# A two-level second product: long VectorE sums moved behind short ones, and the last results stored by quarters

## The chip, the cores and the metric

The kernel runs on one core of a Trainium2 chip. The core has five engines, each with its own queue of instructions: TensorE (PE; its weight loads are shown as PEld), VectorE (DVE), ScalarE (ACT), GpSimd (POOL) and SyncE (SP), which only issues transfers. The engines wait for each other through semaphores; an engine carries out its own queue strictly in order. The metric is the device time of one execution in microseconds; of several executions the median is taken.

## The reference

Attention with normalised queries and keys, followed by a feed-forward block with a squared ReLU, all in 32-bit floats:

```
q_n, k_n = rmsnorm(q, g_q), rmsnorm(k, g_k)          # 8 batches, 12 heads, 448 positions, 64 wide
attn = softmax(q_n @ k_n.T / sqrt(64))
x = (attn @ v) -> (3584, 768)                        # 8 * 448 rows, 12 * 64 columns
h = x @ w_in                                         # (3584, 2048)
out = (maximum(h, 0) ** 2) @ w_out                   # (3584, 768)
```

The last line is the second product. The change concerns its last part alone.

## The kernel before, in words

The eight batches are worked in four spans of two. In each span attention fills `xT`, the first product turns it into `gT` (sixteen chunks of 128 rows of the hidden layer, and 2 x 448 columns, one half for each batch), and the second product turns `gT` into output. Both products use a scheme with seven block products in place of eight: the matrices are cut into two by two blocks, and sums and differences of blocks are multiplied. The sums of weights are made once; the differences of activations for the second product are made by `combine` (L1021), four VectorE subtractions of 128x448 for each chunk, which fill `gC` and one half of `gT`. In the first three spans the second product runs beside the attention of the next span. For the last span there is no attention left, and `last_product` (L1144) does it. It is the function that changes.

`last_product` goes through the seven block products in the order A11, A12, S2, S1, S3, A22, S4 (L1148), here called block product 0 to 6, and each of them is done by the same scheme a second time, on blocks of half the size. Each has three row blocks of 128 output rows (m = 0, 1, 2). Row blocks 0 and 1 are done by the inner scheme; row block 2 ("third", L1228) is a plain product. For one block product TensorE runs, in this order, eight groups: `pa` (a11 b11), `ps` (row block 2, sixteen matmuls of 448 columns), `pb` (s2 t2), `pc` (s1 t1), `pd` (s3 t3), and then adds onto three of these: `pa` again (a12 b21), `pd` again (a22 t4), `pc` again (s4 b22). Each of the small groups has eight matmul records of 224 columns. An accumulator that is added onto has to be read in between, where its first content alone is needed:

- L1261: ScalarE copies the first `pa` to `p1i`;
- L1273 and L1277: VectorE makes `zi` from `p1i` and `pb`, and `yi` from `zi` and the first `pc`;
- L1283 to L1287: VectorE's `meet` (its work stands at L1244) takes the first `pd` into the second half of row block 1; only then may the second `pd` group start, since it adds onto the same bank;
- L1290 or L1292, L1294, L1300: the same for the second `pa`, `pd` and `pc`. These are 128x224 and short.

The long VectorE work is `add_g(o, n)` (L1185, its subtraction at L1191): for each block product o four differences t1 to t4 of 128x896, from the eight chunks of that block's activations. They alternate between two sets of places, so those of block product o + 1 may be made while o runs. The sums of weights s1 to s4 of the next block product are GpSimd's (`add_weights`, L1173, its work at L1179), and the weights themselves come by one transfer of 1.5 MB (`load_set`, L1168, issued by SP).

The order in the queues is the order of the program text: nothing reorders it. Ahead of `last_product`'s first group, in the last two steps of the last first_product, VectorE is given add_g(0, 0) to add_g(0, 3) and half of combine for the last chunk (L1387 to L1393). Then each block product o gives it, in this order: add_g(o + 1, 0) to (o + 1, 2) (L1262), the stores held over from the block product before, row block 2's sum (L1238), `zi`, `yi`, add_g(o + 1, 3) (L1278), and the `meet`s. The other half of that combine follows at the end of block product 0 (L1308).

Finished output leaves by `deliver` (L1137): VectorE transposes a 128x448 tile in squares of 32 into `osb` (L1139), and four transfers of 32 partitions each write it out (L1142). In block product 6 (`end`) the transfers alternate between the queues of SP and ScalarE, row block 1 is stored as a whole once both its halves are done, and row block 0 in two halves (L1296 to L1303).

Of the kernel before, what the change touches and what calls it, by code (L numbers as in the profile page):

```python
# [387 lines left out]
def attention_then_ffn_bounded(  # L388
# [37 lines left out]
    B, H, S, D = q.shape  # L426
# [9 lines left out]
    HF = NFC // 2  # L436
# [23 lines left out]
    def bank(name, n=None):  # L460

        turn[0] += n is None
        return ps_m.tile([P, S], F32, tag="mn"[turn[0] % 2 if n is None else n], name=name)
# [557 lines left out]
    def combine(f, parts=(0, 1)):  # L1021


        g11, g12 = gT[:, f, 0:S], gT[:, f, S:2 * S]
        g21, g22 = gT[:, HF + f, 0:S], gT[:, HF + f, S:2 * S]
        sub = nc.vector.tensor_tensor
        if 0 in parts:
            sub(gC[:, 0, f], g12, g11, ALU.subtract)
            sub(gC[:, 1, f], g22, gC[:, 0, f], ALU.subtract)
        if 1 in parts:  # L1030
            sub(gC[:, 2, f], g21, gC[:, 1, f], ALU.subtract)
            sub(g12, g22, g12, ALU.subtract)
# [111 lines left out]
    def last_product(pool):  # L1144
# [4 lines left out]
        HK, HS = HF // 2, S // 2  # L1149
# [7 lines left out]
        ts = [[t[:, n * NT2:(n + 1) * NT2].rearrange("p (c n) -> p c n", c=HK) for n in range(4)] for t in (cf, xf)]  # L1157
        dead = [gT[:, f, 0:S] for f in range(HF)] + [gC[:, 1, f] for f in range(HF)]
        late = []
        sub, add = ALU.subtract, ALU.add  # L1160

        def weights_of(o, m, k):
            return sets[o % 2].rearrange("p (k c n) -> p k c n", k=2, c=HK)[:, k, :, m * P:(m + 1) * P]

        def sums_of(o):
            return [t.rearrange("p (c n) -> p c n", c=HK) for t in left[o % 2]]
# [14 lines left out]
        def parts_of(o):  # L1181
            rhs = rhs_of[order[o]]
            return [[rhs[:, k * HK:(k + 1) * HK, t * HS:(t + 1) * HS] for t in range(2)] for k in range(2)]

        def add_g(o, n):  # L1185
            if o == len(order):
                return
            (b11, b12), (b21, b22) = parts_of(o)
            t1, t2, t3, t4 = ts[o % 2]
            dst, x, y = ((t1, b12, b11), (t2, b22, t1), (t3, b22, b12), (t4, b21, t2))[n]  # L1190
            nc.vector.tensor_tensor(dst, x, y, sub)  # L1191

        def small_of(name):
            return work.tile([P, HS], F32, tag=name, name=name, bufs=1)
# [8 lines left out]
        def run(ps, lhs, rhs, first=True):  # L1203
            for c in range(HK):
                nc.tensor.matmul(ps, lhs[:, c], rhs[:, c], start=first and c == 0, stop=c == HK - 1,  # L1205
                                 skip_group_check=not first)

        turn[0] += 1
        for o, i in enumerate(order):
            end = o + 1 == len(order)  # L1210
            (b11, b12), (b21, b22) = parts_of(o)
            (a11, a12), (a21, a22) = [[weights_of(o, m, k) for k in range(2)] for m in range(2)]
            s1, s2, s3, s4 = sums_of(o)
            t1, t2, t3, t4 = ts[o % 2]

            into = {A11: [(None, p1s)], A12: [(p1s, None)], S2: [(p1s, p1s)], S1: [(p1s, ys)],
                    S3: [(ys, None), (p1s, p1s)], A22: [(p1s, None)], S4: [(ys, None)]}[i]
            leaves = any(dst is None for _, dst in into)
            into = [(base, dst or homes[i]) for base, dst in into]
            at = ((HC if i in (S3, A22) else 0), 1 if i in (S3, S4) else 0)  # L1220

            def send(m, part=slice(0, S // 32)):
                deliver(work, NSPAN - 1, into[0][1][m], m + at[0], at[1],
                        (nc.sync, nc.scalar) if end else (nc.sync,), part, 5)

            both = len(into) > 1

            def third():  # L1228
                m = HC - 1
                ps = bank("ps")  # L1230
                for c in range(HF):
                    nc.tensor.matmul(ps, weights_of(o, m, c // HK)[:, c % HK], rhs_of[i][:, c],  # L1232
                                     start=c == 0, stop=c == HF - 1)
                for base, dst in into:
                    if base is None:
                        nc.scalar.copy(dst[m], ps)
                    else:
                        nc.vector.tensor_tensor(dst[m], base[m], ps, add)  # L1238

            def meet(m, t, left, ps):  # L1240

                part = slice(t * HS, (t + 1) * HS)
                dst = blocks[m] if both else into[0][1][m]
                nc.vector.tensor_tensor(dst[:, part], left, ps, add)  # L1244

            def based(m, t, x, name):
                base = into[0][0]
                if both or base is None:
                    return x
                y = small_of(name)  # L1250
                nc.gpsimd.tensor_tensor(y, x, base[m][:, t * HS:(t + 1) * HS], add)
                return y

            def settle(m):
                for base, dst in into if both else ():
                    nc.gpsimd.tensor_tensor(dst[m], base[m], blocks[m], add)

            pa = ps_s.tile([P, 2, 512], F32, tag="s", name="pa")[:, 0, 0:HS]
            run(pa, a11, b11)
            p1 = small_of("p1i")  # L1260
            nc.scalar.copy(p1, pa)  # L1261
            for n in range(3):  # L1262
                add_g(o + 1, n)
            for args in late:
                deliver(*args)
            late[:] = []
            third()
            if leaves:
                send(HC - 1)
            pb = ps_o.tile([P, S], F32, tag="o", name="pb")[:, 0:HS]  # L1270
            run(pb, s2, t2)
            z, y = small_of("zi"), small_of("yi")
            nc.vector.tensor_tensor(z, p1, pb, add)  # L1273
            z21, z12 = based(1, 0, z, "za"), based(0, 1, z, "zb")
            pc = bank("pc")[:, 0:HS]
            run(pc, s1, t1)
            nc.vector.tensor_tensor(y, z, pc, add)  # L1277
            add_g(o + 1, 3)  # L1278
            pd = ps_o.tile([P, S], F32, tag="t", name="pd")[:, 0:HS]
            run(pd, s3, t3)  # L1280
            add_weights(o + 1)
            if both or into[0][0] is None:
                meet(1, 1, y, pd)  # L1283
            else:
                meet(1, 1, into[0][0][1][:, HS:S], pd)
                x = into[0][1][1][:, HS:S]
                (nc.vector if end else nc.gpsimd).tensor_tensor(x, x, y, add)  # L1287
            run(pa, a12, b21, False)
            if both or into[0][0] is None:
                nc.scalar.copy((blocks if both else into[0][1])[0][:, 0:HS], pa)  # L1290
            else:
                meet(0, 0, into[0][0][0][:, 0:HS], pa)  # L1292
            run(pd, a22, t4, False)
            meet(1, 0, z21, pd)  # L1294
            settle(1)
            if end:  # L1296
                send(1)
                send(0, slice(0, HS // 32))
            run(pc, s4, b22, False)
            meet(0, 1, z12, pc)  # L1300
            settle(0)
            if end:
                send(0, slice(HS // 32, S // 32))  # L1303
            elif leaves:
                for m in (1, 0):
                    late.append((work, NSPAN - 1, into[0][1][m], m + at[0], at[1], (nc.sync,), slice(0, S // 32), 5))
            if o == 0:
                combine(HF - 1, (1,))  # L1308
            load_set(o + 2)
        yield  # L1310

# [66 lines left out]
    with tc.tile_pool(name="last_product", bufs=2, reuse_waits="tile") as last:  # L1378
        rest = last_product(last)
        load_set, add_weights, add_g = next(rest)  # L1380
        with tc.tile_pool(name="first_product", bufs=2, reuse_waits="tile") as work:
            for u, _ in enumerate(first_product(work, NSPAN - 1)):
                if u in (14, 21):
                    load_set(u // 7 - 2)
                if u == N1 // 2:
                    add_weights(0)
                if u == N1 - 2:  # L1387
                    add_g(0, 0)
                    add_g(0, 1)
                if u == N1 - 1:  # L1390
                    add_g(0, 2)
                    add_g(0, 3)
                    combine(HF - 1, (0,))  # L1393
        with tc.tile_pool(name="second_product", bufs=2, reuse_waits="tile") as work:
            rest.send(work)

# [2 lines left out]
def kernel(  # L1399
# [49 lines left out]
    with tc.If(bits <= limit) as small_scores:  # L1449
        with tc.manual_schedule():  # L1450
            attention_then_ffn_bounded(tc, *args, held)
# [32 lines left out]
```

## Time and profile before

| what | time |
|---|---|
| median of 7 runs | 1359.15 us (1357.55 to 1360.98) |
| profiled execution, its own time | 1363.34 us |
| its span, first to last instruction | 1361.0 us |
| granted TensorE clock, mean | 0.995 |
| TensorE busy / VectorE busy | 1333.8 us / 877.5 us |
| first matmul of last_product | 1230.23 us after the span's start |
| first matmul of block product 1 | 1251.47 us |
| first matmul of block product 6 | 1334.84 us |
| last VectorE instruction | 1352.14 to 1352.55 us |

All times inside the kernel are counted from the span's start, in one profiled execution. The page of the profile lists how long each engine was busy, then the chain of work that ended last, followed back from the last instruction: the share of an engine or line in it says how much of the time it decided. The timeline has a row for each instruction, or run of like ones, with the idle time before it and the instruction that ended that idle time in brackets. A table of stages gives the busy time of each engine in a stretch of time, and then PEclk, the share of full clock that TensorE was granted in it. For transfers, "to landing" is the time from issue to completion.

### The profile page before, as it was taken

The page shows a single profiled execution, that of the slowest core. Times are in us where ns is not written, and L with a number is a line of the kernel's source. Part 1 is how long each engine was busy: PE and PEld are TensorE (multiplying, and loading weights), DVE is VectorE, ACT ScalarE, POOL GpSimd, SP SyncE. Part 2 cuts the span into 40 slices and gives each one's busy share as a digit, 9 for nine tenths or more (in the row PEclk, how much of TensorE's full clock was granted, in tenths as well). Part 3 has the DMA queues.
Part 4 walks back from the last instruction along what each step waited for, and adds up shares of the span by engine and source line. Part 5 has one row for each costly group of instructions (what it writes and reads, how often), then busy time and mean ns, then how long its engine had stood idle before and what let it go on. Part 6 is the DMA issues. An engine that isn't in the chain of part 4 may idle for free.

```text
span 1361.0 us, 17239 instructions
## 1 busy us (share of the span) xinstructions
PE 1333.8 (98%) x5770; PEld 670.6 (49%) x5770; DVE 877.5 (64%) x1536; ACT 431.7 (32%) x681; POOL 620.2 (46%) x504
## 2 busy tenths in 40 slices
PE   7999999999999999999999999999999999999997
PEld 3333445444444455444444455444444445556886
DVE  5999788599987433568787623457788733336552
ACT  6877466533332012233332111223333211110000
POOL 5666533455664122646555222446556312323452
PEclk8999999999999999999999999999999999999999
DMA  9687899656676333355685432345665435321333
GB/s 237 186 255 198 287 367 328 191 123 116 131 155 127 101 88 88 100 119 105 145 152 119 114 94 87 98 106 124 135 126 117 107 97 167 100 81 47 113 103 54
DMA packets 413814, 190.15 MB, mean 140 GB/s; under 512 B 282388, under 2 KB 408724, under 8 KB 413716
## 3 DMA queue, kind: packets, MB, share of 16 engines
q1 hardware_dynamic: 406164, 180.21, 51.4%
q0 software_dynamic: 4736, 8.40, 2.4%
q8 instruction: 48, 0.79, 0.2%
q10 hardware_dynamic: 2816, 0.34, 0.2%
q14 instruction: 50, 0.41, 0.1%
HBM read 155.72 MB, written 33.16 MB: 139 GB/s over the span
## 4 chain that ended last, share of the span: by engine, by line
PE 88%; DVE 6%; ACT 2%; DMA 1%; issue 1%; POOL 0%; SPq 0%; DVEq 0%; POOLq 0%; ACTq 0%
PE ps L1106 28%; PE pd L1068 10%; PE pa L1068 10%; PE pc L1068 10%; PE sc L785 7%; PE pav L862 7%; PE pb L1068 5%; PE ps L1232 3%; PE pd L1205 2%; PE pc L1205 1%; PE pa L1205 1%; DVE gT L810 1%; ACT gT L797 1%; DMA gT<-in_moe_w_in_dram 1%; PE tot L876 1%
## 5 line engine op out<-in xcount | busy, mean ns | idle before, releaser
L1106 PE MATMUL ps<-gT,sw 128*128 128x448 f32 x576 | 225.8, 543 | 0.0
L1044 POOL TENSOR_TENSOR gT<-gT 128x448 f32<-128x448 f32 x96 | 94.1, 982 | 285.2 <-ACT gT L1040 285.2
L750 POOL TENSOR_TENSOR half<-half,mhalf 128x28 f32<-128x28 f32 x36 | 174.9, 4857 | 71.9 <-DVE half L749 68.6
L1106 PE MATMUL ps<-gC,sw 128*128 128x448 f32 x432 | 170.1, 543 | 0.0
L1106 PEld LDWEIGHTS ps<-gT,sw 128*128 128x128 f32 x576 | 107.5, 190 | 113.9 <-issue 110.3
L1068 PE MATMUL pa<-xT,sw 128*128 128x448 f32 x384 | 155.0, 540 | 0.6 <-ACT p L1072 0.6
L1040 ACT ACTIVATE gT<-gT 128x448 f32<-128x448 f32 x96 | 55.4, 577 | 313.5 <-DVE gT L1083 313.5
L1106 PEld LDWEIGHTS ps<-gC,sw 128*128 128x128 f32 x432 | 80.6, 190 | 86.3 <-issue 83.7
L787 ACT ACTIVATE pr<-sc 128x896 f32<-128x896 f32 x87 | 77.4, 915 | 124.0 <-PE sc L785 124.0
L785 PE MATMUL sc<-qkT 64*64 64x448 f32 (+1 forms) x1152 | 109.8, 496 | 0.0
L1068 PEld LDWEIGHTS pa<-xT,sw 128*128 128x128 f32 x384 | 72.8, 190 | 72.7 <-issue 70.6
L583 POOL TENSOR_TENSOR gC<-gC 128x384 f32<-128x384 f32 x64 | 76.2, 1208 | 62.2 <-DVE gC L579 60.4
L1083 DVE TENSOR_TENSOR gT<-z,pd 128x448 f32<-128x448 f32 x32 | 19.8, 620 | 97.8 <-PE pd L1068 97.6
L1068 PE MATMUL pd<-xT,sw 128*128 128x448 f32 x192 | 77.9, 542 | 1.3 <-DVE z L1075 1.3
L830 POOL DMA_DIRECT2D xT<-factors x72 | 38.0, 532 | 90.5 <-DMA factors<-square 54.4
L1068 PE MATMUL pd<-xC,sw 128*128 128x448 f32 x192 | 77.5, 540 | 1.3 <-DVE gT L1083 1.3
L1068 PE MATMUL pb<-xC,sw 128*128 128x448 f32 x192 | 77.5, 540 | 0.1
L1068 PE MATMUL pc<-xC,sw 128*128 128x448 f32 x192 | 77.4, 539 | 0.0
L1068 PE MATMUL pc<-xT,sw 128*128 128x448 f32 x192 | 77.4, 539 | 0.0
L752 POOL TENSOR_TENSOR qk<-qk,half 128x448 f32<-128x448 f32 x72 | 75.6, 1070 | 2.8
L862 PE MATMUL rest<-pr,vt 64*64 64x448 f32 x348 | 72.7, 537 | 0.0
L862 PE MATMUL pav<-pr,vt 64*64 64x448 f32 x348 | 72.7, 537 | 0.0
(233 smaller groups left out, 2167.5 us busy)
## 6 DMA issues: line engine op xcount, KB each, us to landing
sw<-w1s SPq DMA_DIRECT2D x224, 192.0 KB, 2.3
sw<-w2s SPq DMA_DIRECT2D x126, 256.0 KB, 3.3
w1s<-gC SPq DMA_DIRECT2D x8, 1344.0 KB, 7.2
w2s<-gC SPq DMA_DIRECT2D x8, 1344.0 KB, 6.3
out_dram<-osb SPq DMA_DIRECT2D x184, 56.0 KB, 1.8
qk<-in_q_dram SPq DMA_DIRECT2D x144, 56.0 KB, 3.7
qk<-in_k_dram SPq DMA_DIRECT2D x144, 56.0 KB, 3.0
xT<-factors POOLq DMA_DIRECT2D x72, 112.0 KB, 3.4
```

The lines of the kernel that those rows point to most:

```text
L583: nc.gpsimd.tensor_tensor(*[blocks_of(n)[:, place_of(n, i)] for i in (dst, x, y)], op)
L750: nc.gpsimd.tensor_tensor(half, half, mhalf, ALU.pow)
L752: nc.gpsimd.tensor_tensor(qkn[:, s], raw[:, s], half[:, s * NG:(s + 1) * NG].rearrange("p g -> p g ()").to_broadcast([P, NG, 32]), ALU.mult)
L785: nc.tensor.matmul(sc[part, h, 0:n], qkT[rows, 0, 1, keys], qkT[rows, 0, 0, of], start=True, stop=True)
L787: nc.scalar.activation(pr, sc[:, :, 0:n], AF.Exp)
L862: nc.tensor.matmul(into, vs[i][rows, h, c, :], probs[i, c][rows, h, :], start=(c == 0), stop=(c == NF), skip_group_check=True)
L1040: nc.scalar.activation(g, src, AF.Relu)
L1044: nc.gpsimd.tensor_tensor(g, g, g, ALU.mult)
L1068: nc.tensor.matmul(ps, stream[n + at][:, c], rhs[:, c], start=first and c == 0, stop=c == HC - 1, skip_group_check=not first)
L1106: nc.tensor.matmul(ps, stream[n][:, c % 4], rhs_of[i][:, c], start=c == 0, stop=c == HF - 1)
L1205: nc.tensor.matmul(ps, lhs[:, c], rhs[:, c], start=first and c == 0, stop=c == HK - 1, skip_group_check=not first)
L1232: nc.tensor.matmul(ps, weights_of(o, m, c // HK)[:, c % HK], rhs_of[i][:, c], start=c == 0, stop=c == HF - 1)
```

## The change

It has two parts. In block product 0 the long differences for block product 1 go behind the first `meet` that a TensorE group waits for, all four together, and the whole combine of the last chunk goes to the end of block product 0. In the later block products the order is as it was. In block product 6 row block 1 is delivered in two halves, too: its second half as soon as it is summed, its first half behind the second `pd`; the first half of row block 0 goes out behind the second `pa`. `former` and `latter` are the two halves of the 448 columns.

```
+        former, latter = slice(0, HS // 32), slice(HS // 32, S // 32)
...
             nc.scalar.copy(p1, pa)
-            for n in range(3):
+            for n in range(3 if o else 0):
                 add_g(o + 1, n)
...
             nc.vector.tensor_tensor(y, z, pc, add)
-            add_g(o + 1, 3)
+            if o:
+                add_g(o + 1, 3)
...
                 (nc.vector if end else nc.gpsimd).tensor_tensor(x, x, y, add)
+            if end:
+                send(1, latter)
+            if o == 0:
+                for n in range(4):
+                    add_g(1, n)
             run(pa, a12, b21, False)
             if both or into[0][0] is None:
                 nc.scalar.copy((blocks if both else into[0][1])[0][:, 0:HS], pa)
             else:
                 meet(0, 0, into[0][0][0][:, 0:HS], pa)
+            if end:
+                send(0, former)
             run(pd, a22, t4, False)
             meet(1, 0, z21, pd)
             settle(1)
             if end:
-                send(1)
-                send(0, slice(0, HS // 32))
+                send(1, former)
             run(pc, s4, b22, False)
             meet(0, 1, z12, pc)
             settle(0)
             if end:
-                send(0, slice(HS // 32, S // 32))
+                send(0, latter)
...
             if o == 0:
-                combine(HF - 1, (1,))
+                combine(HF - 1)
...
                 if u == N1 - 1:
                     add_g(0, 2)
                     add_g(0, 3)
-                    combine(HF - 1, (0,))
```

More of the change, by code (lines that the diff above doesn't have):

```diff
@@ L1159, in last_product @@
         late = []
+        former, latter = slice(0, HS // 32), slice(HS // 32, S // 32)
         sub, add = ALU.subtract, ALU.add
@@ L1261, in last_product @@
             nc.scalar.copy(p1, pa)
-            for n in range(3):
+            for n in range(3 if o else 0):
                 add_g(o + 1, n)
@@ L1277, in last_product @@
             nc.vector.tensor_tensor(y, z, pc, add)
-            add_g(o + 1, 3)
+            if o:
+                add_g(o + 1, 3)
             pd = ps_o.tile([P, S], F32, tag="t", name="pd")[:, 0:HS]
@@ L1287, in last_product @@
                 (nc.vector if end else nc.gpsimd).tensor_tensor(x, x, y, add)
+            if end:
+                send(1, latter)
+            if o == 0:
+                for n in range(4):
+                    add_g(1, n)
             run(pa, a12, b21, False)
@@ L1292, in last_product @@
                 meet(0, 0, into[0][0][0][:, 0:HS], pa)
+            if end:
+                send(0, former)
             run(pd, a22, t4, False)
@@ L1296, in last_product @@
             if end:
-                send(1)
-                send(0, slice(0, HS // 32))
+                send(1, former)
             run(pc, s4, b22, False)
@@ L1302, in last_product @@
             if end:
-                send(0, slice(HS // 32, S // 32))
+                send(0, latter)
             elif leaves:
@@ L1307, in last_product @@
             if o == 0:
-                combine(HF - 1, (1,))
+                combine(HF - 1)
             load_set(o + 2)
@@ L1392, in attention_then_ffn_bounded @@
                     add_g(0, 3)
-                    combine(HF - 1, (0,))
         with tc.tile_pool(name="second_product", bufs=2, reuse_waits="tile") as work:
```

## The prediction

> **What bounds the kernel now.** I read the page from its first part to its fourth, then the chain of waits through the last 150 us, then the timeline there. TensorE (PE) is busy for 98% of the span and holds 88% of the chain that ended last, so an edit to VectorE (DVE) or to the stores pays only where PE waits, or after PE's last matmul.
>
> ```profile
> PE 1333.8 (98%) x5770; PEld 670.6 (49%) x5770; DVE 877.5 (64%) x1536; ACT 431.7 (32%) x681; POOL 620.2 (46%) x504
> ...
> PE 88%; DVE 6%; ACT 2%; DMA 1%; issue 1%; POOL 0%; SPq 0%; DVEq 0%; POOLq 0%; ACTq 0%
> ```
>
> The change touches one span of about 22 us at the start of the last product and the last 18 us. The waits between 1240 and 1253 us, and then the timeline (start, duration, engine, line, operation, idle time before and who ended it), show the first place:
>
> ```profile
> PE pd L1205 <- DVE p L1244: 2.7, 1, 2.7
> ...
> 1236.00 1.71 DVE L1028 TENSOR_TENSOR gC<-gT 128x448 f32<-128x448 f32 x1
> 1237.75 1.58 DVE L1029 TENSOR_TENSOR gC<-gT,gC 128x448 f32<-128x448 f32 x1
> 1239.25 2.19 DVE L1191 TENSOR_TENSOR xT<-gT 128x896 f32<-128x896 f32 x1
> 1241.47 2.04 DVE L1191 TENSOR_TENSOR xT<-gT,xT 128x896 f32<-128x896 f32 x1
> 1243.43 1.08 DVE L1191 TENSOR_TENSOR xT<-gT 128x896 f32<-128x896 f32 x1
> 1244.43 0.38 DVE L1273 TENSOR_TENSOR zi<-p1i,pb 128x224 f32<-128x224 f32 x1
> 1244.91 0.39 DVE L1277 TENSOR_TENSOR yi<-zi,pc 128x224 f32<-128x224 f32 x1
> 1245.22 1.08 DVE L1191 TENSOR_TENSOR xT<-gT,xT 128x896 f32<-128x896 f32 x1
> 1246.22 0.38 DVE L1244 TENSOR_TENSOR p<-yi,pd 128x224 f32<-128x224 f32 x1
> 1246.66 2.74 PE L1205 MATMUL pd<-xC,qk 128*128 128x224 f32 x8 [2.68 <-DVE p L1244]
> ```
>
> DVE works without a gap. Five long sums (two of combine, three of add_g) stand ahead of the short zi, a fourth add_g ahead of the short L1244, and PE's second pd group may not start before L1244 has read pd. What the wait does to the clock is in the stages (PE, PEld, DVE, ACT, POOL busy, then PEclk):
>
> ```profile
> 1246.66:1251.47 4.81, 4.81 (x16) 4.49 (x17) 0.39 (x1) 0.00 (x0) 0.00 (x0) 0.65 0.20 29
> 1251.47:1253.20 1.73, 1.73 (x10) 1.71 (x10) 1.53 (x4) 0.01 (x1) 0.00 (x0) 1.00 0.97 387
> ```
>
> The 16 matmuls behind the wait took 4.81 us at a granted clock of 0.65; at 1.00 a group of eight takes 1.51 us, as the chain gives for nearly every other group. The second place is behind the last matmul:
>
> ```profile
> 1350.62 0.94 DVE L1139 STREAM_TRANSPOSE osb<-gT 128x448 f32<-128x448 f32 x2
> 1351.72 0.39 DVE L1244 TENSOR_TENSOR gT<-zb,pc 128x224 f32<-128x224 f32 x1 [0.15 <-PE pc L1205]
> 1352.14 0.41 DVE L1139 STREAM_TRANSPOSE osb<-gT 128x224 f32<-128x224 f32 x1
> ...
> L1142 SPq DMA_DIRECT2D out_dram<-osb x6: 315/397/1734, 1351.3 to 1356.2; - x6
> L1142 ACTq DMA_DIRECT2D out_dram<-osb x6: 374/465/1682, 1351.3 to 1355.0; - x6
> ...
> DMA to landing us min/median/max: 1.9/3.1/3.9
> ```
>
> DVE is done at 1352.55, yet SP issues until 1356.2 and the span ends at 1361.0: twelve stores, four of them (row block 1) of 56 KB, come within 5 us on two queues, and one issue on each queue took 1.7 us.
>
> **The change part by part.**
>
> *Long sums behind the short ones.* Nothing is removed: the same four add_g and four combine instructions run later. In the new DVE order zi follows add_g(0,3), which ends at 1234.26 + 1.82 = 1236.08. From then on the short ones wait for PE alone. In the third block product zi starts 1.78 us after pb's first matmul (1277.49 against 1275.71), yi 1.71 us after pc's (1278.93 against 1277.22). Here that makes zi 1237.76 + 1.78 = 1239.54, yi 1239.28 + 1.71 = 1240.99, and L1244 1240.79 + 1.71 = 1242.50, done by 1242.9. PE can start the second pd group at 1242.30 + 1.51 = 1243.81, so 0.9 us of slack replaces the wait. Gain: 1246.66 - 1243.81 = 2.85 us of waiting, and 4.81 - 2 x 1.51 = 1.79 us of slow clock. Together 4.6 us; the next block product starts at 1246.84 and not at 1251.47.
>
> Bounds for this term: the wait itself is certain to have been paid, 2.85; the clock part is 0 if other executions do not lose clock there, 1.79 if they do. I take 4.6, from the one execution that can be seen. The Trainium skill ("TensorE: Matmul & The Clock Gate", section "What's actually happening") says that the clock halves after an idle window of about 3.4 us, in windows that run freely. An idle time of 2.85 us falls short of that, so by the page the clock part need not be there and the whole change would come to 5.4 us by the terms below; the row shows 0.65 after 2.85 us, and I go by the row.
>
> What is late next: add_g(1,0) to (1,3) start at 1242.9. GpSimd (POOL), beside which a long sum took 2.0 to 2.2 us and alone 1.08, has its last add_weights until 1242.56 in this trace, earlier if DVE idles beside it, and then waits 18.68 us for zi:
>
> ```profile
> 1240.44 2.12 POOL L1179 TENSOR_TENSOR qkT<-wb,xT 128x512 f32<-128x512 f32 x1
> ...
> 1261.25 0.66 POOL L1251 TENSOR_TENSOR za<-zi,p 128x224 f32<-128x224 f32 x1 [18.68 <-DVE zi L1273]
> ```
>
> So 4 x 1.09 gives 1247.3. The two short L1244 of the second pd and pc groups are queued behind and end at 1248.1. PE does not wait for them: their banks are next written in the following block product, about 10 us later. combine's four sums at 0.54 apart end at 1250.3, three add_g at 1.05 at 1253.4. Then L1238 is wanted, 6.29 us after the third-row group starts (1259.27 against 1252.98): 1246.84 + 1.51 + 6.29 = 1254.6. Slack 1.2 us. Sums that PE reads in the next block product (its pb group, at 1254.4) are ready by 1247.3. combine's results are read one block product later still. Cost: none, at worst as in rival 4. On SP's queue the load of the next weight set, issued when the second pd group ended (1249.48), moves with that group; nothing is put ahead of it, and POOL needs it only after zb. POOL's queue keeps its order.
>
> *Quarters at the end.* Row block 1 is transposed and stored in two halves, the first right behind L1287; the first half of row block 0 goes behind the first pa sum. DVE: one transpose of 0.65 becomes two of 0.41, +0.17 us, all in gaps: 1347.92 to 1348.35 ahead of L1244 at 1348.62; 1349.0 to 1349.46 ahead of 1350.20; 1350.62 to 1351.03 ahead of 1351.72. The last transpose still ends at 1352.55. Stores: four of 56 KB become eight of 28 KB, so 16 in place of 12, eight on SP and eight on ACT, in four bursts of two per queue from 1348.4, 1349.5, 1351.1 and 1352.6. A burst takes 0.32 to 0.48 an issue, so each queue is free again before the next burst. ACT has no other work left.
>
> Last issue: 1352.58 + 0.44 = 1353.0, against 1356.2. With the shortest time to landing for both, 1.9, the gain is 3.2 us. With 2.6, the median over the last 20 us, for the new one alone it is 2.5. With one 1.7 us issue on the queue it is about 1.5; with two in a row, 0. I take 2.5: the queue is emptier than the rows that show 3.1 to 3.9, and busier than the shortest. From landing to the end, 2.9 us, all stays. The bounds are 0 and 3.2; a loss is excluded only if no queue falls behind (rival 4 has the other engine's version).
>
> The Trainium skill ("DMA: Bandwidth & Descriptors", section "Rules for kernel authors") speaks against this part: coalesce small transfers, under 64 KB one pays mostly overhead. With its fixed 2.0 us per transfer and two more on each queue in series, 4.0 us would be lost, and the whole would be a gain of 0.6 us. Here stores of 56 KB follow each other every 0.5 us on one queue while each takes 1.9 or more to land, so the overhead overlaps, and I go by the rows.
>
> **Sum.** 4.6 + 2.5 = 7.1 us. The profiled execution goes from a span of 1361.0 to 1353.9 and from 1363.34 (2.3 around the span) to 1356.2. It stands 4.2 above the median of the seven runs, 1359.15; I carry the difference over: 1352.0.
>
> **The rivals.**
>
> 1. *The tail gives nothing* (10%): a slow issue or a late landing holds the last store anyway. For it: the 1.7 us issues, whose cause the rows do not name. Against: half the bytes are out 2 to 3 us sooner. 1359.15 - 4.6 = 1354.5.
> 2. *The slow clock is not in the timed runs* (11%): the profiled execution is the slowest of all seen, and the clock's loss may depend on when the gap falls. 1359.15 - 2.85 - 2.5 = 1353.8.
> 3. *The change does not do what it says in the first block* (5%): PE's second pd group is held by something that the late L1244 hid. Against: the weights and t4 that it reads were ready by 1236.1. Only the tail is left: 1356.7.
> 4. *Slower* (5%): the sums put behind the short ones come back as a wait in the second block product. Place: DVE between 1242.9 and the L1244 ahead of that block's second pd group. If POOL ran beside all of them, 4 x 2.19 + 2 x 0.39 + 4 x 1.71 + 3 x 2.19 = 23 us would end at 1265.9, 11.3 later than L1238 is wanted. PE would wait some 10 us there and lose 1.8 of clock: 11.8 - 7.1 = 4.7 slower, 1363.9. It costs from 1.2 us of delay on, and outweighs the gains from about 8. Against it: POOL's 18.68 us without work.
>
> **How the numbers follow.** The forecast has 69%, its own range 1350.4 to 1354.0 (tail 3.2 down to 1.5, and 0.9 each way, half of what the seven runs reach from their middle). With rivals 1 and 2 that is 90%, and they set the upper end: 1355.6, which leaves the tail at 0 and part of the clock. Seven runs spread over 0.25%; a difference of 0.2%, 2.7 us, is about what can be told from none. Under 1356.4 counts as faster: the forecast and rivals 1 and 2, 90%, less 2 for their worst ends: 88. Rival 3 and those ends: 7. Rival 4: 5.
>
> **What will show it.** Right: L1244 some 0.9 us before the second pd group, which starts with no wait; PEclk 1.00 through the first block product; the four add_g at about 1.09 each behind it; the next block product 16.6 us after the first; the last store issued within 0.5 us of the last transpose's end. Wrong: a PE wait on t2, on L1244 or on a bank in the second block product; long sums at 2 us; store issues over 1 us in the last burst; or a clock below 1.00 elsewhere. A timed gain near 5 with a profiled one near 7 would be rival 2.

## The result, and the profile after

The changed kernel takes 1356.08 us (median of 15 runs, 1354.28 to 1358.81), the kernel before 1359.26 us (37 runs). The ratio is 0.9974, with a 95% interval from 0.9968 to 0.9981: 2.6 to 4.3 us faster. The forecast was 7.1 us faster, with a range that ended at 1355.6: the direction held, the size did not. The profiled execution took 1358.08 us, its span 1355.8.

The page of the changed kernel, first and fourth part: TensorE's busy time is 1.2 us shorter, and its share of the chain went from 88% to 90%.

```profile
PE 1332.6 (98%) x5770; PEld 669.6 (49%) x5770; DVE 872.8 (64%) x1537; ACT 432.0 (32%) x681; POOL 620.1 (46%) x504
...
PE 90%; DVE 5%; ACT 3%; issue 1%; ACTq 0%; DVEq 0%
```

The timeline of the changed kernel in block product 0, VectorE and TensorE (start, duration, engine, line, operation, idle time before and who ended it; L1192 is the line of add_g now, L1245 that of `meet`):

```profile
1238.28 0.39 DVE L1274 TENSOR_TENSOR zi<-p1i,pb 128x224 f32<-128x224 f32 x1 [3.47 <-PE pb L1206]
1239.72 0.39 DVE L1278 TENSOR_TENSOR yi<-zi,pc 128x224 f32<-128x224 f32 x1 [1.05 <-PE pc L1206]
1241.24 0.39 DVE L1245 TENSOR_TENSOR p<-yi,pd 128x224 f32<-128x224 f32 x1 [1.12 <-PE pd L1206]
1241.54 1.09 DVE L1192 TENSOR_TENSOR xT<-gT 128x896 f32<-128x896 f32 x1
1242.55 1.68 PE L1206 MATMUL pd<-xC,qk 128*128 128x224 f32 x8
1242.73 1.09 DVE L1192 TENSOR_TENSOR xT<-gT,xT 128x896 f32<-128x896 f32 x1
...
1253.37 0.62 DVE L1239 TENSOR_TENSOR gT<-p,ps 128x448 f32<-128x448 f32 x1 [1.43 <-PE ps L1233]
```

The short sums now wait for TensorE, and the second pd group starts 0.92 us after L1245 has ended, with no idle time before it. The long sums take 1.09 us. The row block 2 sum of the next block product finds VectorE idle for 1.43 us, so the backlog is gone by then. The stage behind it (PE, PEld, DVE, ACT, POOL busy, then PEclk) ran at full clock:

```profile
1242.55:1247.09 4.54, 4.54 (x25) 4.54 (x25) 4.40 (x8) 0.35 (x1) 0.00 (x0) 1.00 0.37 96
```

The end went the other way. SP's waits in the last 20 us (total, times, longest), and the stores of the four small bursts:

```profile
SPq L1142 <- DMA out_dram<-osb: 10.5, 3, 4.9
...
L1142 ACTq DMA_DIRECT2D out_dram<-osb x8: 322/458/1403, 1342.5 to 1347.0; - x8
L1142 SPq DMA_DIRECT2D out_dram<-osb x8: 316/417/1550, 1345.5 to 1351.0; - x8
```

Each burst gives two stores to each queue, and the first burst's transpose ended at 1342.46. ScalarE issued its first store at 1342.5, SP only at 1345.5: SP waited 10.5 us in these 20 for other stores to land: 4.9 ahead of its first store of row block 2, 4.8 ahead of its first small store, 0.8 later on. The first two waits began before there was anything to store; counted from ScalarE's first store of the same data, SP was 1.9 and 3.0 us late. In the kernel before the same row reads 1.5 us, in a window of about the same length:

```profile
SPq L1142 <- DMA out_dram<-osb: 1.5, 2, 1.2
```

Where the 5.2 us between the two spans are, by the timelines:

| stretch | before | after | difference |
|---|---|---|---|
| to the first matmul of last_product | 1230.23 | 1228.97 | -1.3 (not touched by the change) |
| block product 0, first matmul to that of block product 1 | 21.24 | 16.61 | -4.6 |
| from there to the end of the last transpose | 101.1 | 101.1 | 0.0 |
| end of the last transpose to the end of the span | 8.45 | 9.2 | +0.7 |

The first row is not the change's: TensorE's hundredth matmul, some 31 us into the span, already comes 1.5 us sooner. Such differences appear between executions of one kernel: a stretch at half clock of 3.4 us costs 1.7 us, and the first 30 us had from none to two of them in the fourteen executions profiled, whatever the kernel. These two executions had two each, so the 1.3 us have another cause, which stays open. The change itself comes to -4.6 + 0.7 = -3.9 us here, inside the measured interval.

### The profile page after: what moved, and what is told of

Same layout as the page of the kernel before. It is cut to its first block, busy times and chain, and to the rows that moved or that the text cites. A ratio compares the mean times of both kernels' runs of the same rounds, so it can differ in the third digit from the quotient of the medians.

```text
span 1355.8 us, 17250 instructions
## 1 busy us (share of the span) xinstructions
PE 1332.6 (98%) x5770; PEld 669.6 (49%) x5770; DVE 872.8 (64%) x1537; ACT 432.0 (32%) x681; POOL 620.1 (46%) x504
## 4 chain that ended last, share of the span: by engine, by line
PE 90%; DVE 5%; ACT 3%; issue 1%; ACTq 0%; DVEq 0%
PE ps L1106 29%; PE pd L1068 10%; PE pa L1068 10%; PE pc L1068 10%; PE sc L785 7%; PE pav L862 7%; PE pb L1068 5%; PE ps L1233 3%; PE pd L1206 2%; PE pc L1206 2%; PE pa L1206 2%; ACT gT L797 1%; PE sc L793 1%; DVE gT L810 1%; PE pb L1206 1%
```

## The experiments

Theory A: the wait and its slow clock were paid as forecast, and the quarters lost time in place of winning it, because SP's stores wait for ScalarE's. The transfers of the two queues count their landings on eight semaphores, dealt out in turn; a store may not be issued until the last one on its semaphore has landed. The built programs list the order in which they are dealt out. In the change, from the first small burst on (queue and semaphore):

```
ACT 5, ACT 6, SP 7 (row block 2), ACT 0, ACT 1, SP 2 (row block 2), ACT 3, ACT 4,
SP 5, ACT 6, SP 7, ACT 0, SP 1, SP 2, SP 3, SP 4, SP 5, SP 6
```

SP's first small store, on semaphore 5, has to wait for ScalarE's first small store; its later ones wait for ScalarE's on 1, 3 and 4. The trace of the change agrees: ScalarE's store on semaphore 5 landed at 1345.44 and SP's was issued at 1345.50; on semaphore 3 it was 1349.24 and 1349.31. Theory B: the slow clock is not paid in most timed runs, and the quarters change nothing. Theory C: the small stores themselves hold the tail, whatever the semaphores.

**The reordering alone.** The change without its new and split `send`s:

```
-            if end:
-                send(1, latter)
...
-            if end:
-                send(0, former)
...
             if end:
-                send(1, former)
+                send(1)
+                send(0, former)
```

> The reordering of VectorE's work in block product 0 alone; the last block product stores as before (row block 1 whole, row block 0 in halves). Theory A (the wait and its slow clock are paid in the timed runs as in the profiled one; what is missing from the forecast was lost by the quarters): 4.6 us faster than before, ratio 0.9966, and about 0.7 us faster than the change. Theory B (the slow clock behind the wait is not paid in most timed runs): 2.9 us faster, ratio 0.9979, and no faster than the change. Profile: no wait ahead of the second pd group of block product 0 by both.

Measured: 1354.55 us, ratio 0.9962 (0.9947 to 0.9976), 5.2 us faster; B's 0.9979 is outside. No wait, block product 0 in 16.60 us, and 8.4 us from the last transpose to the end, as before.

**The quarters alone.** The kernel before, with the new `send`s and VectorE's old order.

> The quarters alone; VectorE's order in block product 0 as before. Theory A: 0.7 us slower than before (ratio 1.0005), from the end of the last transpose to the end of the span 9.1 us against 8.45, and SP's stores wait for the landing of ScalarE's stores that count on the same semaphore. Theory B: 0.3 us faster or the same (ratio 0.9998 to 1.0).

Measured: 1360.78 us, ratio 1.0004 (0.9992 to 1.0015). The timing cannot tell 0.5 us from none, and it rules out the forecast gain of 2.5 us (0.9982). The profile has the wait on the stores, and 8.8 us from the last transpose to the end:

```profile
SPq L1142 <- DMA out_dram<-osb: 10.6, 3, 4.9
```

**The change, with the semaphores in order.** The stores held over from block product 5 alternate between the queues:

```
-                    late.append((work, NSPAN - 1, into[0][1][m], m + at[0], at[1], (nc.sync,), slice(0, S // 32), 5))
+                    late.append((work, NSPAN - 1, into[0][1][m], m + at[0], at[1], (nc.sync, nc.scalar) if o + 2 == len(order) else (nc.sync,), slice(0, S // 32), 5))
```

The queues then alternate through the last bursts (ACT 7, SP 0, ACT 1, SP 2, ACT 3, SP 4, ...), and each semaphore comes back to the queue it was on, two bursts later.

> The change, and in addition the stores held over from block product 5 alternate between SP's and ScalarE's queues. Nothing else moves, but the eight semaphores of the stores are then dealt out so that a store of the last block product shares its semaphore only with a store two bursts earlier on its own queue. Theory A: SP's stores no longer wait for ScalarE's; the last store is issued within 0.6 us of the last transpose and the tail is 2.5 us shorter than before: 6 to 7 us faster than before (ratio 0.9950 to 0.9956). Theory C (the small stores themselves, or a slow DMA engine, hold the tail, whatever the semaphores): as the change, 3.2 to 3.9 us faster, and store issues above 1 us in the last burst.

Measured: 1354.05 us, ratio 0.9953 (0.9937 to 0.9968), 6.4 us faster than before. The stores and SP's waits:

```profile
L1142 SPq DMA_DIRECT2D out_dram<-osb x8: 315/450/1510, 1339.3 to 1343.8; - x8
L1142 ACTq DMA_DIRECT2D out_dram<-osb x8: 322/450/1904, 1339.3 to 1346.1; - x8
...
SPq L1142 <- DMA out_dram<-osb: 0.2, 1, 0.2
```

Both queues start together (1339.3, and 1342.5 against 1345.5 in the change), SP's wait fell from 10.5 us to 0.2, and from the last transpose (ended 1343.42) to the end are 6.7 us, 1.8 less than before. That is A, but not all of the 2.5: a store on each queue still took over 1.5 us to issue in the last burst, and ScalarE's last went out 2.7 us after the last transpose. That last store also waited 0.8 us for ScalarE's own store on its semaphore, issued at 1342.16 and landed at 1346.10: semaphores in order couple a queue with itself. Two transfers of 16 KB of the kind "instruction" run near the end of every profile looked at, some 3.5 us before the end of the last transpose and within 0.5 us of it. Here they took 1.3 and 1.2 us, and the four issues of more than 1 us stand beside them, two by each. That the one holds the other is an inference from their places; no run moved them.

**The change again**, on the same chip as these three.

> The change itself once more, beside the three on the same chip. All theories: 2.6 to 4.3 us faster than before, as measured (ratio 0.9968 to 0.9981). Theory A: slower than the order alone by 0.7 us; theory B: the same as it.

Measured: 1355.80 us, ratio 0.9969 (0.9958 to 0.9980). By the medians it lies 1.3 us behind the reordering alone, whose interval overlaps its own, and 1.8 us behind the version with the semaphores in order, whose slowest run (1354.98) is faster than seven of these ten. Part of the 1.8 us may be the clock early in the execution: over the whole of it 0.997 to 0.999 was granted there, 0.995 to 0.998 here. The tails after the last transpose do not contain that: 8.8 us here and 9.2 in the first profile of the change, against 6.7.

**All of the last stores on SP's queue.** `(nc.sync,)` for the last block product, too.

> The change, with all stores of the last block product on SP's queue alone. Each semaphore then comes back only after eight stores on the same queue, so no store waits for a store that was just issued elsewhere; but four stores of a burst follow each other on one queue, about 0.5 us apart. Theory A (the shared semaphores hold the tail): last store issued about 1.6 us after the last transpose, 4.3 in the change; 1 to 2 us faster than the change, ratio to before 0.9955 to 0.9962. Theory C (issue rate, small transfers or a slow DMA engine hold the tail): one queue in place of two makes it 1 to 2 us slower than the change, ratio 0.9977 to 0.9985.

Measured: 1356.71 us, ratio 0.9976 (0.9967 to 0.9985). A's number is outside. C's range lies inside, but so does the ratio of the change itself, so the times do not tell this version from the change; its tail is 9.5 us against 9.2. The row says why nothing was won:

```profile
L1142 SPq DMA_DIRECT2D out_dram<-osb x16: 315/444/1386, 1339.5 to 1348.5; - x16
```

Sixteen stores at about 0.5 us and two slow issues fill the queue from the first burst on: a burst of four takes longer than the 1.1 to 1.6 us to the next. A's expectation had looked at the last burst by itself. So a queue's issue time is a limit of its own. It also keeps SP late in the change: SP loses 3.0 us at the first burst, and from there to its last issue are 5.5 us: about 0.5 us for each store, 1.1 more for one slow issue of 1.55 us, and 0.9 of waiting for ScalarE's store on semaphore 3.

**Halves, with the semaphores in order.** The reordering alone, with the same edit of `late`.

> The reordering, the old stores of the last block product (row block 1 whole, row block 0 in halves), and the held-over stores alternating between the queues, so that the semaphores come round in order as in the third experiment. It tells what the quarters are worth once no store waits for one on the other queue. Theory A: 2.5 us of the tail belongs to quarters and semaphores together, so this is 1 to 2 us slower than the third experiment (ratio to before 0.9960 to 0.9966). Rival: the quarters are worth nothing, the same as the third experiment (0.9953).

Measured: 1354.94 us, ratio 0.9966 (0.9954 to 0.9978), 7.6 us of tail against 6.7 with the quarters. As A has it: the quarters are worth about 1 us once the semaphores come round in order. The two ratios' intervals overlap, so this rests on one profile of each.

**Combine's half alone moved back.** VectorE's other long sums stay; only this moves to the end of block product 0:

```
-                    combine(HF - 1, (0,))
...
-                combine(HF - 1, (1,))
+                combine(HF - 1)
```

> The kernel before with combine's half alone moved to the end of block product 0; the four long sums stay where they were. If what matters is that VectorE's backlog ahead of L1244 is under 2.85 us shorter, then L1028 and L1029 (1.75 + 1.50 us from start to start) are enough by themselves: L1244 ends 0.4 us or more before PE wants it, no wait, and the next block product starts 16.6 us after the first. If the long sums run slower than they did, a wait of up to 1 us is left.

In the one execution, which was profiled, the second case came: 0.8 us of waiting is left, and block product 0 takes 17.70 us. Three of the long sums moved up beside GpSimd's add_weights, and took 2.0 to 2.2 us each:

```profile
1234.32 2.19 DVE L1191 TENSOR_TENSOR xT<-gT 128x896 f32<-128x896 f32 x1
1236.61 1.98 DVE L1191 TENSOR_TENSOR xT<-gT,xT 128x896 f32<-128x896 f32 x1
1238.52 2.17 DVE L1191 TENSOR_TENSOR xT<-gT 128x896 f32<-128x896 f32 x1
...
1243.12 1.21 PE L1205 MATMUL pd<-xC,qk 128*128 128x224 f32 x5 [0.82 <-DVE p L1244]
```

**The four long sums alone moved back**, combine as before.

> The kernel before with the four long sums for block product 1 moved behind L1244, and combine's half left where it was. combine's two sums end about 3.2 us after add_g(0, 3), before pb is done, so zi, yi and L1244 wait for PE alone: no wait ahead of the second pd group, and the next block product 16.6 us after the first.

In the one execution: no wait, 16.61 us for block product 0. This half of the edit is enough for the whole of the first gain.

**The fourth long sum alone moved**, add_g(1, 3) behind L1244, for the clock; and the same kernel once more, and the kernel before once more.

> The kernel before with one of the four long sums, add_g(1, 3), moved behind the L1244 ahead of the second pd group; stores as before. The wait of PE there falls from 2.85 us to about 1.85. If any wait of this kind costs a window of half clock, the gain is 1.0 us (ratio 0.9993) and the record of the clock shows one half-clock stretch of 3.4 us behind the wait. If the wait has to fill most of a window of 3.4 us, the half-clock stretch is gone in most executions and the gain is 1.0 + 1.7 = 2.7 us (ratio 0.9980).

> A second look at the kernel with a wait of 1.85 us ahead of the second pd group, for the clock alone. If 1.85 us of waiting is too short to cost clock, there is again no stretch of half clock behind it; if it depends on when the wait falls in windows that run freely, there may be one of 3.4 us.

> A second look at the kernel before, for the clock behind its wait of 2.7 to 2.85 us. Theory A: a stretch of half clock of 3.4 us right behind it, as in the first look and in the second experiment. Theory B: none.

Timed: ratio 0.9993 (0.9984 to 1.0002), 1.0 us faster, with 0.3 slower to 2.2 faster inside: nearer to a clock that is paid in most executions (1.0) than to one that is not (2.7, outside). The stage behind the wait, first in the first look, then in the second, then in the kernel before:

```profile
1243.25:1247.90 4.65, 4.65 (x25) 4.65 (x26) 2.65 (x5) 0.00 (x0) 0.00 (x0) 1.00 0.33 90
```

```profile
1243.60:1249.80 6.20, 6.20 (x24) 5.88 (x25) 2.52 (x5) 0.00 (x0) 0.00 (x0) 0.72 0.29 78
```

```profile
1242.30:1247.10 4.80, 4.75 (x16) 4.46 (x17) 0.39 (x1) 0.00 (x0) 0.00 (x0) 0.64 0.11 13
```

Behind 1.85 us of waiting the clock was full once (block product 0 in 18.72 us) and halved once behind 1.88 us (20.43, 1.71 more), of the very same program. Behind the longer wait it was reduced in all three profiles that have it: 0.65 in the first of the kernel before, 0.64 here, and 0.68 with the quarters alone. For a wait of 2.7 us no execution without it was seen. What decides it at 1.9 us stays open. Behind the wait the half clock held for 3.41 us, as it did early in the same execution; the two stretches in the second look:

```profile
21.75:25.16 3.41, 3.41 (x11) 1.08 (x8) 3.22 (x6) 1.72 (x5) 0.21 (x1) 0.50 1.09 348
1243.72:1247.13 3.41, 3.41 (x10) 3.09 (x10) 1.13 (x2) 0.00 (x0) 0.00 (x0) 0.50 0.00 0
```

They start 358 lengths of 3.413 us apart. Where that step is counted on from each execution's early stretch (the first look has one from 21.41), the length just before the stretch behind the wait, 1240.31 to 1243.72, holds the whole wait of 1.88 us, and in the first look the length from 1239.97 to 1243.39 holds the whole wait of 1.85 us. So it was not that one of the two waits was split over two lengths.

**Two of four stores on GpSimd's queue**, in the first two small bursts of the version with the semaphores in order.

```
-                        (nc.sync, nc.scalar) if end else (nc.sync,), part, 5)
+                        ((nc.sync, nc.scalar) if m == HC - 1 or (m, part) == (0, latter) or (m, part) == (1, former) else (nc.sync, nc.gpsimd, nc.scalar, nc.gpsimd)) if end else (nc.sync,), part, 5)
```

> The third experiment, with two of the four stores of each of the first two small bursts (second half of row block 1, first half of row block 0) on GpSimd's queue, which counts on semaphores of its own. If issues on two queues at 0.5 us and returns of the same eight semaphores are what is left of the tail, the last store is issued earlier than the 2.7 us after the last transpose of the third experiment, and the kernel is 0.5 to 1.5 us faster than it (ratio to before 0.9942 to 0.9950). If the slow issues of 1.5 us in the last burst are what is left, it is the same as the third experiment (0.9953).

Measured: 1356.84 us, ratio 0.9977 (0.9967 to 0.9988), slower than the third experiment by about 3 us, which neither expectation has. The stores did what was hoped: the last was issued 0.45 us after the last transpose. The last line of the kernel shows what came in its place:

```profile
L1486 SPq EVENT_SEMAPHORE  x14: 17/28/28, 1348.6 to 1354.8; - x14
L1486 POOLq EVENT_SEMAPHORE  x4: 17/17/17, 1353.8 to 1354.8; - x4
L1486 POOLq DRAIN  x3: 40/107/9619, 1344.1 to 1354.6; - x3
```

GpSimd closes with a drain of 9.6 us. It started at 1344.1, behind GpSimd's last store, and ended at 1353.7, where GpSimd's closing semaphore stands; SP had gone through the store semaphores from 1348.6 on. In the third experiment the same drain took 9.3 us from 1338.4 and was over at 1347.7, before SP was done. There the stores bound the end; here the drain does.

## Why the prediction was wrong

- *The wait and the clock: right in the profiled executions, and the timed ones agree.* Forecast 4.6 us, measured 4.63 in the profile, and 5.2 (3.3 to 7.2) for the reordering alone in time. The working held in its parts: zi 1.78 us after pb's first matmul, 0.92 us of slack against 0.9, long sums of 1.09 us, 1.43 us of idle time ahead of the row block 2 sum against 1.2. One reading was loose: the 2.85 us, which it calls an idle time, are how late the group started; the row has 2.68 us of idle time. That the clock's part was paid at all rested on one profiled execution; two more behind a wait of 2.7 us, and 5.2 us in time, bear it out. The Trainium skill ("TensorE: Matmul & The Clock Gate", section "What's actually happening") asks for an idle window of about 3.4 us before the clock halves; the row was the better guide, since a wait of 1.88 us was followed by the half clock as well.
- *The tail: the step that failed.* The prediction put "each queue is free again before the next burst", and from it "Last issue: 1352.58 + 0.44 = 1353.0", a gain of 2.5 us between bounds of 0 and 3.2. Measured: the last store went out 4.3 us after the last transpose (0.45 forecast, 3.65 before), and the tail is 0.7 us longer in the change and 0.3 with the quarters alone. The lower bound of 0 was wrong as well. What was missing is the wait of a store on the semaphore of the other queue's store, with the 0.5 us an issue that keeps a late queue late. It could have been read beforehand: the row of SP's waits on `out_dram` (1.5 us before) and the order of the semaphores in the built program were there. The prediction looked at durations of issues and at time to landing, not at what an issue waits for. Something smaller is left besides: with the semaphores in order the tail is still 0.7 us longer than a gain of 2.5 us would have made it. There stand the slow issues of the last burst (1.57 and 1.51 us), which the prediction had named as a sign of being wrong and which the change has too (1.40 and 1.55 us), and ScalarE's 0.8 us of waiting for its own store; how the 0.7 us divide between them is not shown.
- *The sum.* 4.6 - 0.7 = 3.9 us against the 2.6 to 4.3 measured. With the tail at its measured value the forecast would have been 1355.3; the median is 0.8 above.
- *The rivals.* Rival 1 (the tail gives nothing) named the right place, and was 1.6 us off; the loss that it did not allow is 0.7 of that. Rival 2 was half right: the half clock depends on the execution, but it was there behind every wait of 2.7 us that was profiled. Rival 3 and rival 4 did not come: there is no new wait of TensorE in block product 0 or 1, and GpSimd was idle for 15.6 us ahead of its next sum.
- *The rule on small transfers* (the Trainium skill, "DMA: Bandwidth & Descriptors", section "Rules for kernel authors") had the sign of the tail right, but its reason, the overhead of each transfer, is not what these runs show: with the semaphores in order, the same small stores end 0.9 us sooner behind the last transpose than the larger ones (6.7 against 7.6 us, one profile of each). The fixed 2.0 us that the prediction took from that page is its fit for transfers issued from GpSimd; these are issued by SP and ScalarE.

The version with the semaphores in order, 1354.05 us on a chip where the kernel before took 1360.01 and the change 1355.80, is the fastest measured here.

## What to carry to other kernels

When long and short work share an engine's queue, add up the backlog ahead of the short instruction that another engine waits for; here the slack, read from a later, undisturbed pass of the same loop, and with it the gain in the profile came out within 0.1 us. Before splitting stores over two queues, read in the built program which earlier transfer each one must wait for: shared semaphores coupled the queues here, and a queue that started a burst 3.0 us late stayed late at 0.5 us an issue. Look also at what else ends the program: a faster tail is worth nothing beyond the last engine's closing drain.

## What the runs showed of the hardware that was not expected

- GpSimd's closing drain took 9.3 us in the kernel before and the change, and 9.6 us after its own stores. In the fourteen profiles it started 1.3 to 1.8 us after GpSimd's last work, so late work on GpSimd, however short, can set the end of a kernel.
- The half clock behind a short wait belongs to the execution: the same program waited 1.85 and 1.88 us, and ran on at a PEclk of 1.00 and of 0.72 in the stage behind. It cost 1.71 us.
- Every one of the last stores that took 1 us or more to issue (1.1 to 1.9 us) overlapped an instruction load of 16 KB, in all fourteen profiles; the others took 0.3 to 1.0 us, and some of these overlapped such a load, too. That the load holds the issue is not shown.
